# The last regroup in two halves, three PSUM tags in turn for the output units, batches in their own order

## The chip, the cores and the metric

The kernel runs on one core of a Trainium2 chip. The metric is device time in microseconds for one execution, from the runtime's measurement; the profiled execution also has a span, the time from the first to the last event that the profiler recorded on the core. The engines are PE (matmul, with its weight loads as a row of its own, PEld), DVE (VectorE), ACT (ScalarE), POOL (GpSimd) and SP (SyncE, which here only issues transfers). Each engine works through its own instructions in order.

## What is computed

A linear attention (feature map exp(x) and exp(-x) of a projection) over 8 batches, 8 heads, 576 positions, head size 64 gives x of shape (8, 576, 512). Then a Fourier layer mixes it over the positions:

```python
X = np.fft.rfft(x, axis=1)                       # 64 lowest modes are kept
Yr = einsum('bmd,mde->bme', Xr, w_r) - einsum('bmd,mde->bme', Xi, w_i)
Yi = einsum('bmd,mde->bme', Xr, w_i) + einsum('bmd,mde->bme', Xi, w_r)
Y[:, :n_modes] = Yr + 1j * Yi
y = np.fft.irfft(Y, n=S, axis=1)
u = x + y
return (u + np.maximum(u @ w_ch, 0.0)).astype(np.float32)
```

Inputs and output are float32; the kernel works in bfloat16 with float32 sums.

## The kernel before

**Attention, and the weights.** 32 steps of attention fill `xs_all` (the attention's output, 5 chunks of up to 128 positions for each of 8 batches) and, by matmul with a cosine and sine matrix, the modes `XT`. Beside them the mode weights (64 modes of 512 x 512, real and imaginary) are loaded by POOL's queue in 32 groups and multiplied: `mode_mm` sums a group of 8 modes and a quarter of the input width into `psY`, `mode_sum` adds the quarters up in `Yacc`, and for the last quarter writes `yst`. The last ten groups (k = 22 to 31) come after the attention.

**What is done beside the last groups.** For each chunk, x times `w_ch` is wanted later: `flip_x` (L637) transposes a pair of chunks, `times_w` (L647) multiplies by `wchb` and ACT stores the product in `xw`. For ten pairs of chunks, called late, `reordered` (L672) permutes the rows of `xs_all` to the order of the output (a matmul with `ident_p` at L679, a copy by ACT at L681), so that x can be added by POOL at the end instead of by PE. The table `late` says which.

**Regrouping.** After each two groups of the last quarter (P = 0 to 3, 16 modes each) `by_batch` (L684) regroups `sY`, which has modes and batches mixed, by batch. Its matmuls give Z = Y times `w_ch` (`mm_z`, L689, 16 matmuls a half, 32 columns each) and R = Y itself (`mm_r`, L695), four batches a half, each batch in 32 partitions. `copy(j)` moves batches j and j + 4 with one instruction of ACT (Z into `zall`, L705) and one of DVE (R into `yall`, L706). In P = 3 the copies are a list of five steps that the last loop takes one at a time: batch 0 (with the first half's matmuls), batch 4 (with the second half's), then j = 1, 2 and 3; of the last, both copies are ACT's.

**The output units.** The output is made in 20 units. A unit has two chunks (`half` False: 128 rows each, 1024 numbers in each partition) or the 64-row fifth chunks of two batches (`half` True, 512 numbers). A unit runs so:

- `add_xw` (L760): PE puts `xw` into the PSUM tile `psB` (2 matmuls);
- `add_z` (L768): PE adds the inverse transform of `zall` (2 matmuls, L771), then ACT writes Relu(psB) into the output tile `of` (L773);
- `spec` (L775): PE puts x into `psA` (2 matmuls, L780; left out in a late unit) and adds the inverse transform of `yall` (2 matmuls, L783); DVE adds psA to `of` (L786); in a late unit POOL then adds x from `xs_all` to `of` (L790);
- SP issues the stores (L824): 64 partitions each, so two for a unit.

PSUM is held as four tags T0 to T3 of two banks, all eight banks together; a tile of a tag waits until the readers of the tag's last tile are done. psZ and psR of P = 3 hold T0 and T1. Units 0 to 3 take T2 for psB and T3 for psA each time; from unit 4 on even units take (T2, T3) and odd ones (T0, T1). The units go by b = 0 to 3: the chunks of batch b and of batch b + 4, then their fifth chunks (in b = 3 these come first). The stores of a unit that is not late are issued right after it, those of a late unit two units later (`LAG`). An output tile holds four chunks of a batch and has one of three buffers of tag w0 or w1.

Of the kernel before, what the change touches and what calls it, by code (L numbers as in the profile page):

```python
# [10 lines left out]
F32 = mybir.dt.float32  # L11
# [7 lines left out]
B_, H_, S_, D_ = 8, 8, 576, 64  # L19
NMODES = 64  # L20
DMODEL = 512
NCH = 5
# [4 lines left out]
def kernel(  # L27
# [11 lines left out]
    nc = tc.nc  # L39
# [4 lines left out]
    psum = psum_cm.__enter__()  # L44
    pw = ctx.enter_context(tc.tile_pool(name="pw", bufs=3))
# [10 lines left out]
    Yacc = pers.tile([128, 8, DMODEL], F32, name="Yacc")  # L56
# [93 lines left out]
    def weights(k):  # L150
        g, gi = groups[k]
        wt = {}
        for ri, w in ((0, moe_w_r), (1, moe_w_i)):
            t = pw.tile([128, 8, DMODEL], BF16, name=f"w{'ri'[ri]}", tag=f"w{ri}")
            if gi >= 0:
                nc.gpsimd.dma_start(  # L156
                    t, w[8 * gi:8 * gi + 8, g * 128:(g + 1) * 128, :].rearrange("m p e -> p m e"))
            else:
                for x in range(2):
                    mx = 16 * (-1 - gi) + 8 * x  # L160
                    nc.gpsimd.dma_start(
                        t[64 * x:64 * x + 64],
                        w[mx:mx + 8, g * 64:(g + 1) * 64, :].rearrange("m p e -> p m e"))
            wt[ri] = t
        W[k] = wt
# [252 lines left out]
    def mode_sum(k, psY, pb=None):  # L418
        g, gi = groups[k]
        if gi < 0:  # L420
            G = -1 - gi
            if g == 0:
                nc.vector.tensor_copy(Yacc[:, 2 * G:2 * G + 2, :], psY)
            else:
                nc.vector.tensor_tensor(
                    out=Yacc[:, 2 * G:2 * G + 2, :], in0=psY, in1=Yacc[:, 2 * G:2 * G + 2, :],
                    op=ALU.add)
        elif g < 3:
            nc.vector.tensor_tensor(  # L429
                out=Yacc[:, gi, :], in0=psY, in1=Yacc[:, gi, :], op=ALU.add)  # L430
        else:
            yst = pb.tile([128, DMODEL], BF16, name="yst", tag="yst", bufs=2)
            nc.vector.tensor_tensor(out=yst, in0=psY, in1=Yacc[:, gi, :], op=ALU.add)
            return yst
# [82 lines left out]
    with tc.manual_schedule():  # L517
# [15 lines left out]
        for n in range(N + 2):  # L533
# [60 lines left out]
            e = n - (N + 2 - N_EARLY)  # L594
# [28 lines left out]
    psum = ctx.enter_context(tc.tile_pool(name="psumT", bufs=1, space=bass.MemoryType.PSUM))  # L623
# [4 lines left out]
    yall = pb.tile([128, B_, DMODEL], BF16, name="yall", bufs=1)  # L628
    zall = pb.tile([128, B_, DMODEL], BF16, name="zall", bufs=1)
# [3 lines left out]
    todo = list(range(N_EARLY, B_ * NCH, 2))  # L633
    ahead = []
    copies = []
# [11 lines left out]
    def times_w():  # L647
        i, sT = ahead.pop(0)
        ps = psum.tile([128, 2, DMODEL], F32, name="psW", tag="T2")
        for x in range(2):  # L650
            for dc in range(4):
                nc.tensor.matmul(ps[:, x, :], lhsT=sT[:, x, dc, :], rhs=wchb[:, dc, :],  # L652
                                 start=(dc == 0), stop=(dc == 3))
        nc.scalar.copy(xw[:, i - N_EARLY:i + 2 - N_EARLY, :], ps)  # L654

    def pieces(n):
        for _ in range(n):
# [7 lines left out]
                copies.pop(0)()  # L665


    late = {0: ((1, 0), (1, 2)), 1: ((0, 0), (1, 0), (1, 2)), 2: ((0, 0), (1, 0), (1, 2)),
            3: ((0, 0), (0, 2))}
    reorder = sorted((b + 4 * x) * NCH + c for b in range(4) for x, c in late[b])  # L670

    def reordered(tag):  # L672
        i = reorder[0]
# [9 lines left out]

    def by_batch(sY, P):  # L684
        cols = [sY[:, dc].rearrange("p g c -> p (g c)") for dc in range(4)]
        psZ = psum.tile([128, 2, DMODEL], F32, name="psZ", tag="T0")
        psR = psum.tile([128, 2, DMODEL], F32, name="psR", tag="T1")

        def mm_z(h):  # L689
            for dc in range(4):  # L690
                for j in range(4):
                    nc.tensor.matmul(psZ[32 * j:32 * j + 32, h, :], lhsT=cols[dc][:, j + 4 * h::8],
                                     rhs=wchb[:, dc, :], start=(dc == 0), stop=(dc == 3))

        def mm_r(h):  # L695
            for dc in range(4):
                for j in range(4):
                    nc.tensor.matmul(
                        psR[32 * j:32 * j + 32, h, dc * 128:(dc + 1) * 128],
                        lhsT=cols[dc][:, j + 4 * h::8], rhs=ident_b, start=True, stop=True)  # L700

        def copy(j, h=None, one=False):
            r = slice(32 * j, 32 * j + 32)
            bs, hs = (slice(j, None, 4), slice(0, 2)) if h is None else (j + 4 * h, h)
            nc.scalar.copy(zall[32 * P:32 * P + 32, bs, :], psZ[r, hs, :])  # L705
            (nc.scalar.copy if one else nc.vector.tensor_copy)(  # L706
                yall[32 * P:32 * P + 32, bs, :], psR[r, hs, :])

        if P < 3:
            for f in (mm_z, mm_r):  # L710
                for h in range(2):
                    f(h)
            copies.extend([lambda j=j: copy(j) for j in range(4)])
        else:

            copies.extend([lambda: (mm_z(0), mm_r(0), copy(0, 0)),
                           lambda: (mm_z(1), mm_r(1), copy(0, 1)),
                           lambda: copy(1), lambda: copy(2), lambda: copy(3, None, True)])

    with tc.manual_schedule():  # L720
        plan = {22: 3, 23: 3, 24: 2, 25: 2, 26: 2, 27: 1, 28: 2, 29: 1, 30: 1, 31: 0}
        while k_out < 32:
            k = k_out
            gi = groups[k][1]
            while k_in < min(k_out + NW, 32):
                weights(k_in)
                k_in += 1
            yst = mode_sum(k, mode_mm(k, "T3"), pb)
            k_out += 1
            if yst is not None:  # L730
                if ahead:
                    times_w()
                pt = psum.tile([128, 4, 128], BF16, name="ptY", tag="T3")
                for dc in range(4):
                    nc.tensor.transpose(pt[:, dc, :], yst[:, dc * 128:(dc + 1) * 128], ident_b)
                if gi % 2 == 0:
                    sY = pb.tile([128, 4, 2, 128], BF16, name="sY", tag="sY")
                nc.vector.tensor_copy(sY[:, :, gi % 2, :], pt)
                if gi % 2 == 1:
                    by_batch(sY, gi // 2)  # L740
            pieces(plan[k])
            if k <= 24 or k % 2 == 0:
                assert not copies
                for tag in ("T0", "T1"):
                    if reorder:
                        reordered(tag)
            if k == 30:
                times_w()
        assert not todo and not ahead and not reorder and len(copies) == 5

# [37 lines left out]
            nc.gpsimd.tensor_tensor(out=o, in0=o, in1=xs_all[:, i:i + 2, :], op=ALU.add)  # L790

    units = []
    for b in range(4):
        of = [pw.tile([128, 4, DMODEL], F32, name="of", tag=f"w{x}") for x in range(2)]
        o4 = Yacc[:, 2 * b, :]
        us = []
        for x in range(2):
            out_v = out[b + 4 * x].rearrange("(p n) e -> p n e", n=9)
            for c in (0, 2):
                us.append(dict(bc=((b + 4 * x, c), (b + 4 * x, c + 1)), o=of[x][:, c:c + 2, :],  # L800
                               late=(x, c) in late[b], half=False,
                               dmas=[(out_v[:, 5 * jj + c:5 * jj + c + 2, :],
                                      of[x][jj::2, c:c + 2, :]) for jj in range(2)]))
        u4 = dict(bc=((b, 4), (b + 4, 4)), o=o4, late=False, half=True,
                  dmas=[(out[b + 4 * x].rearrange("(p n) e -> p n e", n=9)[:, 4, :],
                         o4[64 * x:64 * x + 64]) for x in range(2)])
        units += [u4] + us if b == 3 else us + [u4]

    with tc.manual_schedule():
        LAG = 2  # L810
        copies.pop(0)()
        for n in range(len(units) + LAG):
            if n < len(units):
                u = units[n]
                u["tags"] = ("T2", "T3") if n % 2 == 0 or n < 4 else ("T0", "T1")
                add_xw(u)
                add_z(u)
                spec(u)
                if copies:
                    copies.pop(0)()  # L820
            for lag, is_late in ((LAG, True), (0, False)):
                if 0 <= n - lag < len(units) and units[n - lag]["late"] == is_late:
                    for dst, src in units[n - lag]["dmas"]:
                        nc.sync.dma_start(dst, src)  # L824

# [29 lines left out]
```

## Time and profile before

| what | us |
|---|---|
| median of 3 runs (lowest, highest) | 462.61 (461.35, 463.44) |
| the profiled execution | 463.39 |
| its span | 461.6 |
| first to last issue of a store (L824) | 422.3 to 457.9 |

Busy time, out of the span: PE 312.4, DVE 298.8, ACT 264.5, POOL 196.3. The transfers' engines are near full until the last weights have come, at about 415 us, and are used in part from there on; the page's second part shows it slice by slice (the last six slices, of 11.5 us each, moved 207, 140, 63, 146, 318 and 293 GB/s). Busy shares over the span say little about the last 45 us; the timeline and windows of that part are what to read.

### The profile page before, as it was taken

To read this page: it belongs to the slowest core of one execution; us is meant where nothing else is said; L and a number is where in the kernel's file an instruction comes from. 1 tells how busy PE (TensorE), PEld (TensorE's weight loads), DVE (VectorE), ACT (ScalarE), POOL (GpSimd) and SP (SyncE) were. 2 spreads that over 40 slices of the span, in tenths; PEclk is the share of its full clock that TensorE was granted. 3 is DMA by queue.
4 is the path that set the end of the run, shared out by engine and by line. 5 is a ranking of instruction groups with operands and counts; after the bars stand their busy time and mean duration, and the time that the engine had idled before them with its cause. 6 is when DMAs were issued, how large, how long until landed. Compare 5 with 4: busy or idle time off the path is not lost.

```text
span 461.6 us, 11115 instructions
## 1 busy us (share of the span) xinstructions
PE 312.4 (68%) x4637; PEld 202.2 (44%) x4637; DVE 298.8 (65%) x418; ACT 264.5 (57%) x531; POOL 196.3 (43%) x246
## 2 busy tenths in 40 slices
PE   1676777745675777667465655576678878868893
PEld 1464655623454555534343433344344544433341
DVE  5688799856988789876555473776322274465674
ACT  3766876743676877855555453756233445655662
POOL 4596395545564256644344332533022113000583
PEclk9997798886978669986678585989799999999898
DMA  8999999999999999999999999999999999981488
GB/s 170 262 254 241 237 218 217 229 206 219 221 225 218 229 218 222 221 223 224 218 208 223 213 218 219 207 208 207 207 207 207 207 207 207 207 140 63 146 318 293
DMA packets 84577, 99.08 MB, mean 215 GB/s; under 512 B 3504, under 2 KB 75824, under 8 KB 84528
## 3 DMA queue, kind: packets, MB, share of 16 engines
q0 software_dynamic: 73872, 74.72, 97.3%
q1 hardware_dynamic: 10496, 23.60, 15.7%
q8 instruction: 36, 0.59, 0.5%
q14 instruction: 13, 0.11, 0.1%
q10 hardware_dynamic: 160, 0.07, 0.1%
HBM read 163.64 MB, written 9.44 MB: 375 GB/s over the span
## 4 chain that ended last, share of the span: by engine, by line
DMA 26%; DVE 25%; issue 19%; PE 16%; ACT 6%; POOL 5%; SPq 2%; DVEq 0%; ACTq 0%; POOLq 0%
DMA wi<-in_moe_w_i_dram 20%; DVE mkq L227 7%; DVE xs_all L330 4%; DMA q<-in_q_dram 4%; DVE nd L316 3%; DVE tB L309 3%; ACT AA L234 3%; PE psNB L299 2%; ACT e L256 2%; PE ptr L178 2%; DVE of L786 2%; SPq L123 2%; DMA kn<-in_k_dram 2%; PE psB L764 1%; POOL vaug L264 1%
## 5 line engine op out<-in xcount | busy, mean ns | idle before, releaser
L264 POOL TENSOR_TENSOR vaug<-vn,ee 128x576 bf16<-128x576 f32 x64 | 72.6, 1152 | 59.9 <-ACT ee L249 53.9
L234 ACT ACTIVATE AA<-psT 128x1024 bf16<-128x1024 f32 x64 | 62.0, 1021 | 44.0 <-PE psT L202 43.5
L156 POOL DMA_DIRECT2D wr<-in_moe_w_r_dram x24 | 21.8, 908 | 115.5 <-PE psY L410 108.3
L256 ACT ACTIVATE e<-mkq 64x4 f32<-64x4 f32 (+1 forms) x128 | 26.4, 206 | 65.8 <-DVE mkq L227 63.5
L238 ACT ACTIVATE AA<-psk 128x1024 bf16<-128x1024 f32 x64 | 61.4, 1009 | 0.0
L410 PE MATMUL psY<-wi,XT 128*32 128x512 bf16 x192 | 25.3, 472 | 25.5 <-DMA wi<-in_moe_w_i_dram 25.5
L410 PEld LDWEIGHTS <-XT 128*32 128x32 bf16 x384 | 17.8, 167 | 51.0 <-issue 42.6
L227 DVE TENSOR_REDUCE mkq<-psk 128x8 f32<-128x1024 f32 x32 | 38.8, 1213 | 1.3 <-PE psk L193 1.3
L790 POOL TENSOR_TENSOR of<-of,xs_all 128x1024 f32<-128x1024 f32 x10 | 21.1, 2130 | 42.2 <-DVE of L786 42.2
L227 DVE TENSOR_REDUCE mkq<-psq 128x8 f32<-128x1024 f32 x32 | 38.9, 1216 | 0.1
L654 ACT CAST xw<-psW 128x1024 bf16<-128x1024 f32 x17 | 17.2, 1013 | 36.4 <-PE psW L652 36.4
L429 DVE TENSOR_TENSOR Yacc<-psY,Yacc 128x512 f32<-128x512 f32 x16 | 11.0, 690 | 40.8 <-PE psY L410 40.7
L184 DVE COPY kT<-ptr 128x640 bf16<-128x640 bf16 x32 | 15.7, 492 | 29.6 <-PE ptr L178 29.6
L410 PE MATMUL psY<-wr,XT 128*32 128x512 bf16 x192 | 24.7, 473 | 14.9 <-DMA wr<-in_moe_w_r_dram 6.4
L280 PE MATMUL kvz<-vaug,AA 64*128 64x65 bf16 x1152 | 29.5, 211 | 7.4 <-POOL vaug L269 5.9
L309 DVE TENSOR_TENSOR tB<-psNB,e 128x650 f32<-128x650 f32 x32 | 26.7, 833 | 11.4 <-PE psNB L299 10.7
L299 PEld LDWEIGHTS <-AA 128*128 128x128 bf16 x640 | 30.3, 113 | 8.3 <-issue 7.7
L652 PE MATMUL psW<-wchb,sT 128*128 128x512 bf16 x136 | 32.2, 379 | 2.1 <-ACT xw L654 2.1
L330 DVE TENSOR_TENSOR xs_all<-nd,rden 128x640 bf16<-128x640 f32 x32 | 30.8, 964 | 1.1
L280 PEld LDWEIGHTS <-AA 64*128 64x128 bf16 x1152 | 25.2, 107 | 12.3 <-issue 8.3
L178 PE MATMUL ptr<-ident_b,k 128*128 128x128 bf16 x160 | 18.4, 263 | 17.2 <-DVE qT L184 16.5
L316 DVE TENSOR_TENSOR nd<-psNA,tB 128x650 f32<-128x650 f32 x32 | 26.7, 835 | 4.1 <-DVE tB L309 0.5
(128 smaller groups left out, 719.6 us busy)
## 6 DMA issues: line engine op xcount, KB each, us to landing
wr<-in_moe_w_r_dram POOLq DMA_DIRECT2D x24, 1024.0 KB, 23.3
wi<-in_moe_w_i_dram POOLq DMA_DIRECT2D x24, 1024.0 KB, 27.5
wr<-in_moe_w_r_dram POOLq DMA_DIRECT2D x16, 512.0 KB, 18.2
wi<-in_moe_w_i_dram POOLq DMA_DIRECT2D x16, 512.0 KB, 20.5
out_dram<-of SPq DMA_DIRECT2D x32, 256.0 KB, 2.4
vn<-in_v_dram SPq DMA_DIRECT2D x24, 288.0 KB, 5.7
q<-in_q_dram POOLq DMA_DIRECT2D x12, 288.0 KB, 19.2
k<-in_k_dram POOLq DMA_DIRECT2D x12, 288.0 KB, 20.2
```

Of the source, the lines that this page charges most:

```text
L227: nc.vector.tensor_reduce(out=o, in_=i, axis=AX.X, op=ALU.max, apply_absolute_value=True)
L234: nc.scalar.activation(AA[:, 0, ab, 0:1024].rearrange("f (x j p) -> f j x p", j=2, p=64), st["psT"].rearrange("f j (x p) -> f j x p", p=64 ...
L238: nc.scalar.activation(AA[:, 1, ab, 0:1024].rearrange("p (c j f) -> p j c f", c=4, j=2), st["psk"], ACT.Exp, scale=sc)
L256: nc.scalar.activation(e2[64 * jj:64 * jj + 64, hh, 0:NCH - jj], mkq[64 * hh:64 * hh + 64, 1, 5 * jj:5 + 4 * jj], ACT.Exp, scale=2.0)
L264: nc.gpsimd.tensor_tensor(out=vaug[:, ab, :, 0:64], in0=st["v"], in1=ee[:, ab, :].unsqueeze(2).to_broadcast([128, 9, D_]), op=ALU.mult,)
L280: nc.tensor.matmul(kvz[:, hh, ab * 65:(ab + 1) * 65], lhsT=AA[r, 1, ab, 128 * j:128 * j + 128], rhs=vaug[r, ab, j, :], start=(j == 0), sto ...
L299: nc.tensor.matmul(p[:, hh, 65 * c:65 * c + 65], lhsT=AA[:, 0, ab, x:x + 128], rhs=kvzF[:, hh, ab * 65:(ab + 1) * 65], start=True, stop=True,)
L309: nc.vector.tensor_tensor(out=tB, in0=st["psNB"], in1=e2.unsqueeze(3).to_broadcast([128, 2, NCH, 65]), op=ALU.mult,)
L316: nc.vector.tensor_tensor(out=nd, in0=st["psNA"], in1=st["tB"], op=ALU.add)
L330: nc.vector.tensor_tensor(out=xo, in0=nd[:, :, :, 0:64], in1=rden.to_broadcast([128, 2, NCH, 64]), op=ALU.mult,)
L410: nc.tensor.matmul(psY[32 * j:32 * j + 32, :], lhsT=XT[:, c0:c0 + 32, m], rhs=wt[ri][:, 2 * j + par, :], start=(par == 0 and ri == 0), sto ...
L652: nc.tensor.matmul(ps[:, x, :], lhsT=sT[:, x, dc, :], rhs=wchb[:, dc, :], start=(dc == 0), stop=(dc == 3))
```

## The change

Nothing before P = 3 changes but the table `late`, which holds other chunks (still ten pairs). After it:

- the last regroup is in two halves: `make(h)` makes one tile `psL` of tag T0, with Z of four batches in its first bank and R in its second. The second half's matmuls come when batch 4 is first wanted, after the eighth unit. `copy_one(b)` moves one batch: Z by ACT, R by DVE, or by ACT in batches 3, 5 and 7. There are eight steps of copies, taken one batch ahead of need;
- the units go in the order of the batches 0 to 7, with the fifth chunks of two batches after each odd batch;
- psB and psA take tags T1, T2, T3 in turn: the tile numbered s = 2n + x takes T(1 + s mod 3);
- the stores of batches 1 to 5 are of four chunks (two stores of 512 KB a batch), issued after the batch's last unit; the others stay at two chunks. Each unit has its own lag: 3 if late, 1 if it closes a batch of 1 to 5 with a unit that is not late, 0 otherwise. There are 30 stores in place of 40.

```diff
-    late = {0: ((1, 0), (1, 2)), 1: ((0, 0), (1, 0), (1, 2)), 2: ((0, 0), (1, 0), (1, 2)),
-            3: ((0, 0), (0, 2))}
-    reorder = sorted((b + 4 * x) * NCH + c for b in range(4) for x, c in late[b])
+    late = {(b, 0) for b in range(1, B_)} | {(2, 2), (4, 2), (6, 2)}
+    reorder = sorted(b * NCH + c for b, c in late)
...
-            copies.extend([lambda: (mm_z(0), mm_r(0), copy(0, 0)),
-                           lambda: (mm_z(1), mm_r(1), copy(0, 1)),
-                           lambda: copy(1), lambda: copy(2), lambda: copy(3, None, True)])
+            last = {}
+
+            def make(h):
+                last[h] = ps = psum.tile([128, 2, DMODEL], F32, name="psL", tag="T0")
+                mm_z(h, ps[:, 0, :])
+                mm_r(h, ps[:, 1, :])
+
+            def copy_one(b):
+                r = slice(32 * (b % 4), 32 * (b % 4) + 32)
+                ps = last[b // 4]
+                nc.scalar.copy(zall[rows, b, :], ps[r, 0, :])
+                (nc.scalar.copy if b in (3, 5, 7) else nc.vector.tensor_copy)(
+                    yall[rows, b, :], ps[r, 1, :])
+
+            for b in range(B_):
+                copies.append(lambda b=b: (make(b // 4) if b % 4 == 0 else None, copy_one(b)))
...
+    for b in range(B_):
+        of = pw.tile([128, 4, DMODEL], F32, name="of", tag=f"w{b % 2}")
+        out_v = out[b].rearrange("(p n) e -> p n e", n=9)
+        whole = 0 < b < 6
+        for c in (0, 2):
+            c0 = 0 if whole else c
+            units.append(dict(bc=((b, c), (b, c + 1)), o=of[:, c:c + 2, :],
+                              late=(b, c) in late, half=False,
+                              lag=3 if (b, c) in late else 1 if whole else 0,
+                              dmas=[(out_v[:, 5 * jj + c0:5 * jj + c + 2, :],
+                                     of[jj::2, c0:c + 2, :]) for jj in range(2)]
+                              if c == 2 or not whole else []))
+        if b % 2:
+            o4 = Yacc[:, b, :]
+            units.append(dict(bc=((b - 1, 4), (b, 4)), o=o4, late=False, half=True, lag=0,
+                              dmas=[(out[b - 1 + x].rearrange("(p n) e -> p n e", n=9)[:, 4, :],
+                                     o4[64 * x:64 * x + 64]) for x in range(2)]))
 
     with tc.manual_schedule():
-        LAG = 2
         copies.pop(0)()
-        for n in range(len(units) + LAG):
+        for n in range(len(units) + 3):
             if n < len(units):
                 u = units[n]
-                u["tags"] = ("T2", "T3") if n % 2 == 0 or n < 4 else ("T0", "T1")
+                u["tags"] = [f"T{1 + (2 * n + x) % 3}" for x in range(2)]
                 add_xw(u)
                 add_z(u)
                 spec(u)
-                if copies:
+                if copies and 8 - len(copies) <= u["bc"][0][0] + 1:
                     copies.pop(0)()
-            for lag, is_late in ((LAG, True), (0, False)):
-                if 0 <= n - lag < len(units) and units[n - lag]["late"] == is_late:
+            for lag in (3, 1, 0):
+                if 0 <= n - lag < len(units) and units[n - lag]["lag"] == lag:
                     for dst, src in units[n - lag]["dmas"]:
                         nc.sync.dma_start(dst, src)
```

## The prediction, made before the changed kernel had run

> **What bounds the kernel now.** I read the chain of waits first, in order of time, then the timeline of the last 45 us engine by engine, then the granted clock in stretches of 3.4 us. The chain:
>
> ```profile
> 391.35 23.62 DMA wi<-in_moe_w_i_dram
> ...
> 415.96 0.70 DVE yst L433
> ...
> 424.17 1.24 DVE of L786
> 425.41 0.04 issue
> 425.45 0.61 PE psA L783 x2
> ...
> 442.83 0.43 PE psB L764 x2
> 443.26 0.43 PE psB L771 x2
> 443.69 0.43 PE psA L783 x2
> ```
>
> Up to 415 us the kernel waits for its last weights. Nothing before that changes except which rows L679 permutes (ten pairs before, ten after, one a step earlier: two matmuls and a 1.01 us ACT copy, hidden under the 23.62 us load and priced at nothing; without that cover it would be 0.43 + 1.01 us). So the tail decides, from the copy of the last sY (ends 417.58) to the end at 461.6. Two regimes: an opening (424 to 431) in which PE and DVE alternate, and a stretch from 431.5 on in which PE runs back to back.
>
> ```profile
> 430.47 0.64 PE L780 MATMUL psA<-xs_all,ident_b 128*64 128x512 bf16 x2 [1.37 <-DVE of L786]
> 435.68 0.59 PE L764 MATMUL psB<-xw,ident_p 128*128 128x512 bf16 x2
> 436.74 1.02 ACT L773 ACTIVATE of<-psB 128x1024 f32<-128x1024 f32 x1 [0.70 <-PE psB L771]
> 437.80 2.52 DVE L786 TENSOR_TENSOR of<-psA,of 128x1024 f32<-128x1024 f32 x2 [0.50 <-ACT of L773]
> ...
> 451.35 4.21 POOL L790 TENSOR_TENSOR of<-of,xs_all 128x1024 f32<-128x1024 f32 x2 [1.03 <-DVE of L786]
> 452.02 1.20 SPq L824 DMA_DIRECT2D out_dram<-Yacc  x2
> 453.50 4.99 SPq L824 DMA_DIRECT2D out_dram<-of  x8
> ```
>
> From these rows: Relu starts 1.06 after a unit's first matmul (435.68 to 436.74) and takes 1.02; the add follows 0.04 later and takes 1.23 alone; so a unit's add ends 3.35 after its first matmul. The last row is the end of the kernel: eight stores issued in one run on SP, the last at 457.89 (L824's rows run from 422.3 to 457.9), 0.63 apart; the span ends 3.7 later. Whatever moves the start of that run moves the end.
>
> ```profile
> 410.20:413.60 3.40, 2.07 (x10) 1.00 0.59 98
> 413.60:417.10 3.50, 1.96 (x22) 1.00 0.05 9
> ...
> 427.30:430.70 3.40, 1.43 (x9) 0.97 0.15 63
> 430.70:434.10 3.40, 3.40 (x11) 0.53 0.55 192
> 434.10:437.50 3.40, 3.40 (x18) 1.00 0.56 194
> ```
>
> Columns: stretch, length, PE busy (instructions), granted clock, DMA share, GB/s. After the one stretch in which PE was busy 42% the clock is halved for 3.4 us, which costs 1.7 us of PE work; after 56% and 61% it is not.
>
> **The change part by part.** *PE work* is the same: ten late units of 6 matmuls x 0.216 = 1.30, six others of 8 x 0.216 = 1.73, four half units of 1.27 (438.36 to 439.63), and twice the 32 small matmuls (1.26: 417.63 to 418.89).
>
> *Opening.* Before, the first four units share one pair of PSUM tags and the second half's matmuls and two-batch copies (1.22 on DVE, 1.00 on ACT) stand among them: first psB at 418.89, sixth at 431.47, 12.58 us. After, three tags rotate, so tile s takes the tag of tile s-3: psB of unit n waits for the add of unit n-2, psA of unit n for the Relu of unit n-1. Copies are of one batch (0.57 ACT, 0.68 DVE). A small loss: Z and R now share one tile, so the first z copy waits for R's matmuls too (419.01 for 418.77) and DVE's copy waits for ACT's (419.62 for 419.01). Laying it out with the durations above, first matmuls fall at 418.90, 420.91, 422.64, 424.55 (waits for the second unit's add), 426.38, and the sixth at 428.01 (waits for the fourth's add): 9.11 us, 3.46 less, of which 1.26 is the second half's matmuls put off.
>
> *Fifteen later units.* Now the price of three tags: S(n+2) >= S(n) + 3.35 + 0.04, that is 1.70 a unit, where a late unit needs only 1.30 of PE. Before, it was psA, 0.86 later, that waited for the add two units back: (3.39 - 0.86)/2 = 1.27 a unit, under 1.30, and the rows from 435 on show no idle PE. First matmuls after: 428.01, 429.30, 431.41 (add), second half 432.92, 434.24, 436.06; 437.64 (add), 438.93, 441.03 (add), 443.28 (add), 445.11; 446.68 (add), 447.98, 450.08 (add), 452.33 (add), 454.16. The waits at 443.28 and 452.33 are longest since for batches 5 and 7 both copies run on ACT (2 x 0.57) ahead of the Relu that the add needs. PE work from 428.01 on: 9 x 1.30 + 3 x 1.73 + 3 x 1.27 + 1.3 = 22.0, against 27.0 laid out: 5.0 us of waits. Before, 431.47 to 454.0 is 22.5 and holds no such waits, only the 1.7 of halved clock. After, PE is never under 76% busy in a 3.4 us stretch, so by the five rows I expect no halving in the tail.
>
> Behind a waiting psB stand all later matmuls in order, the second half's and its own psA's among them; ACT and DVE then wait for those.
>
> The Trainium skill ("Perfetto Trace Analysis", section Matmul Optimizations) speaks against three tags: it wants all eight PSUM banks in use, and after the change the units rotate through six; the page has no price, only the layout above gives one. On the clock, the Trainium skill ("TensorE: Matmul & The Clock Gate", section "What's actually happening") says the gate's 3.4 us window runs free and halves the clock after an idle one; here 42% busy was enough, and by the page's wording the 1.7 us would not be in the time before and the loss would be 3.9 instead of 2.2.
>
> *The end.* The add of the 19th unit (batch 7, c=2) ends at 452.33 + 1.07 + 1.06 + 1.23 = 455.69. SP stands at that unit's store, in order, with the stores of (6,2), o4 and (7,0) behind it, although the Pool add of (6,2) is done at 454.5: again eight issues in one run, from 455.73 instead of 453.50. Pool's last add (454.52 to 456.64) is done before its turn. Last issue 455.73 + 7 x 0.63 = 460.1, for 457.89: **+2.2 us**.
>
> *Stores.* 40 become 30; ten carry 512 KB. No row has such a store; 128 KB and 256 KB ones issue in 0.571 and 0.570, so I take 0.57; the other end is doubling with the bytes, 1.14. Either way nothing: the last large pair is issued near 447.6, and SP next waits until 452.28 (a Pool add). Landing: 256 KB took 2.4, at 410 GB/s twice that is 3.0; bounded above by the 1024 KB loads' 27.5, which would hold only the reuse of an output buffer. I take 3.0. The bytes are no bound: 9.44 MB / 410 GB/s = 23 us of some 36.
>
> *Sum:* opening -3.46, later units 27.05 - 22.5 = +4.5, end of PE +1.0; the run of stores starts one unit's Relu and add behind PE rather than behind a Pool add, +1.2 more. Span 461.61 + 2.2 = 463.8; with 1.78 around it (463.39 measured for this execution) **465.6**. That execution lies 0.8 over the median 462.61. I do not take the 0.8 off: the halved stretch hangs on one 3.4 us window, so other executions may lack it (463.39 - 1.6 = 461.8), and what I lay out for after has none in either case. The same layout applied to before, with the halved stretch put in, gives the last add at 454.43 (row: 454.36) and the last issue within 0.1 us.
>
> **Unknown costs.** Restart of PE after a wait: the rows show 0.04; PEld's waits on issue up to 0.8. At ten waits, 0 to +1.0; I take 0.04 each. Tags freed earlier than the add's recorded end: -1.4 if a third of the 5.0 goes. The level of the median: -0.8 to 0.
>
> **Rivals.** (1) *Not slower:* three tags hold PE less than I count, since Relu and add pipeline closer. For: in the opening the same three tags are a gain. Against: each wait is one PSUM tile with one reader whose end is a row. With no waits 465.6 - 5.0 = 460.6; it decides from waits under 2.8 us (0.19 a unit instead of 0.33). (2) *The halved clock comes in the tail after too,* since some window falls on a wait: a cycle's 0.86 doubles and the next is late by a little, +1.1: 466.7. Against: 76%. (3) *The offset of the profiled execution carries over* (halved clock or not is the same in all executions): 462.61 + 2.2 = 464.8, which is within 0.5%, about what a measurement of this kernel can tell from no change. (4) *The change does nothing it says*, because stores limit the end: against, the stores before the last run had gaps of SP (452.0, then 453.5).
>
> **How the numbers follow.** Forecast 0.62 (time 464.9 to 466.4); rival 1 0.08 (0.05 faster, 0.03 not), rival 2 0.08, rivals 3 and 4 0.22. Slower by over 0.5% (464.9): 0.62 + 0.08 = 0.70; within: 0.22 + 0.03 = 0.25; faster 0.05. Range: 465.6 - 0.8 - 1.4 = 463.4 to 465.6 + 1.1 + 0.6 of restarts = 467.3.
>
> **What would show it.** PE waits for "DVE of" at L775 in about every second unit, some 5 us in all; a sixth first matmul near 428; no clock below 0.9 between 418 and 455; a last run of eight stores from about 455.7. Wrong if PE runs back to back from 428 on, or if the last stores start before 453.5.

## The result, and the profile after

The changed kernel takes 466.07 us (median of 12 executions, 463.52 to 469.58), the kernel before 462.69 (median of 12 beside it, 461.11 to 464.65). The ratio is 1.0074, 95% interval 1.0051 to 1.0098: slower by about 3.4 us. The profiled execution took 466.13, with a span of 464.4.

Two profiles can't be subtracted end to end here, because the last weights arrive at another time in each execution (414.97 before, 416.33 after, though the code that loads them is the same). So everything below is counted from the end of the last copy of `sY`, where the tail begins: 417.58 before, 418.93 after. "Tail" is from there to the issue of the last store. It is 40.3 before and 42.1 after; to the end of the span 44.0 and 45.4. Of the 2.7 us between the two profiled executions (463.39 and 466.13), then, 1.4 lie ahead of the tail and 1.4 in it.

First the chain of waits after, in order of time (start, length, what):

```profile
392.17 24.16 DMA wi<-in_moe_w_i_dram
...
443.10 1.24 DVE of L797
444.33 0.04 issue
444.38 0.59 PE psB L775 x2
444.97 0.45 PE psB L782 x2
445.41 0.02 issue
445.44 1.03 ACT of L784
446.47 0.02 issue
446.49 1.24 DVE of L797
```

Where the chain of before ran through PE alone at this place, it now goes round: add, first matmul two units later, Relu, add. The timeline of PE after shows the same as waits (start, length, what, idle time before and what ended it):

```profile
438.86 0.59 PE L775 MATMUL psB<-xw,ident_p 128*128 128x512 bf16 x2 [0.52 <-DVE of L797]
440.15 0.59 PE L775 MATMUL psB<-xw,ident_p 128*128 128x512 bf16 x2
442.25 0.59 PE L775 MATMUL psB<-xw,ident_p 128*128 128x512 bf16 x2 [0.64 <-DVE of L797]
444.38 0.59 PE L775 MATMUL psB<-xw,ident_p 128*128 128x512 bf16 x2 [0.67 <-DVE of L797]
```

From 438.86 to 442.25 are 3.39 us for two units, as the prediction's layout had it (3.35 + 0.04). And SP's timeline at the end: stores, then a hole, then a run of eight from 456.67 on.

```profile
453.34 1.12 SPq L836 DMA_DIRECT2D out_dram<-of  x2
456.67 1.11 SPq L836 DMA_DIRECT2D out_dram<-of  x2
...
459.16 1.18 SPq L836 DMA_DIRECT2D out_dram<-Yacc  x2
460.44 1.18 SPq L836 DMA_DIRECT2D out_dram<-of  x2
```

The clock of after, in stretches of 3.41 us laid so that the changes of clock in its trace fall on their ends (stretch, length, PE busy with its instructions, granted clock, DMA share, GB/s). The emptiest stretch of its later units has PE busy 2.10 of 3.41, and the clock is halved only after the stretch in which the last matmuls end:

```profile
441.30:444.71 3.41, 2.10 (x10) 1.00 0.85 310
...
454.95:458.36 3.41, 1.22 (x10) 1.00 0.42 167
458.36:461.78 3.42, 0.00 (x0) 0.50 0.97 332
```

### The profile page after: what moved, and what is told of

It is laid out like the page before. It is cut to its first block, busy times and chain, and to the rows that moved or that the text cites. A ratio compares the mean times of both kernels' runs of the same rounds, so it can differ in the third digit from the quotient of the medians.

```text
span 464.4 us, 11105 instructions
## 1 busy us (share of the span) xinstructions
PE 305.5 (66%) x4637; PEld 198.0 (43%) x4637; DVE 299.6 (65%) x419; ACT 264.9 (57%) x536; POOL 196.9 (42%) x246
## 4 chain that ended last, share of the span: by engine, by line
DMA 31%; DVE 24%; issue 18%; PE 11%; ACT 7%; POOL 6%; SPq 1%; POOLq 1%; DVEq 0%; ACTq 0%
DMA wi<-in_moe_w_i_dram 20%; DVE mkq L227 7%; DMA k<-in_k_dram 5%; DMA q<-in_q_dram 4%; DVE xs_all L330 4%; DVE nd L316 3%; DVE tB L309 3%; ACT AA L234 2%; POOL vaug L264 2%; DVE of L797 2%; DMA kn<-in_k_dram 2%; ACT of L784 2%; SPq L123 1%; ACT e L256 1%; PE ptr L178 1%
## 5 line engine op out<-in xcount | busy, mean ns | idle before, releaser
L410 PEld LDWEIGHTS <-XT 128*32 128x32 bf16 x384 | 17.8, 167 | 54.9 <-issue 45.4
L429 DVE TENSOR_TENSOR Yacc<-psY,Yacc 128x512 f32<-128x512 f32 x16 | 11.0, 689 | 42.8 <-PE psY L410 42.7
L330 DVE TENSOR_TENSOR xs_all<-nd,rden 128x640 bf16<-128x640 f32 x32 | 32.8, 1025 | 1.1
L299 PEld LDWEIGHTS <-AA 128*128 128x128 bf16 x640 | 28.0, 108 | 9.5 <-issue 9.1
L202 PE MATMUL psT<-qT,w 64*128 64x512 bf16 x64 | 15.1, 462 | 23.0 <-DVE mkq L227 23.0
```

The lines of the kernel that those rows point to most:

```text
L299: nc.tensor.matmul(p[:, hh, 65 * c:65 * c + 65], lhsT=AA[:, 0, ab, x:x + 128], rhs=kvzF[:, hh, ab * 65:(ab + 1) * 65], start=True, stop=True,)
L330: nc.vector.tensor_tensor(out=xo, in0=nd[:, :, :, 0:64], in1=rden.to_broadcast([128, 2, NCH, 64]), op=ALU.mult,)
L410: nc.tensor.matmul(psY[32 * j:32 * j + 32, :], lhsT=XT[:, c0:c0 + 32, m], rhs=wt[ri][:, 2 * j + par, :], start=(par == 0 and ri == 0), sto ...
```

## The experiments

Each is one edit of one of the two kernels unless it says more. The tails of all, from their profiles:

| kernel | tail | to the end of the span | halved clock that overlaps the tail, up to the last matmul |
|---|---|---|---|
| before | 40.3 | 44.0 | 430.5 to 433.9 |
| before, second profile | 38.7 | 42.4 | none |
| after | 42.1 | 45.4 | none |
| store order | 40.9 | 44.2 | none |
| fourth tag | 41.2 | 44.8 | 417.8 to 421.2 |
| copies on DVE | 41.8 | 45.1 | none |
| small stores | 42.1 | 45.8 | none |
| before, three tags | 42.7 | 46.4 | 431.4 to 434.8 |
| four tags, more edits | 40.2 | 43.7 | 416.1 to 419.5 |
| one store a unit | 39.3 | 43.7 | 416.6 to 423.4 |
| filled wait | 38.5 | 42.1 | none |
| no fill | 40.5 | 44.2 | 415.9 to 422.8 |
| after, filled wait | 42.1 | 45.4 | none |

### The price of three tags alone, in the kernel before

```diff
-                u["tags"] = ("T2", "T3") if n % 2 == 0 or n < 4 else ("T0", "T1")
+                u["tags"] = ("T2", "T3") if n < 4 else [f"T{1 + (2 * n + x) % 3}" for x in range(2)]
```

> The kernel before with one edit: from the fifth unit on psB and psA take T1, T2, T3 in turn instead of the pairs (T2, T3) and (T0, T1). Opening, copies, order and stores are those of before. Theory: this is the price of three tags alone, PE waits for the add two units back in the later units: tail 40.3 (before, with a stretch of halved clock) or 38.7 (before without it) plus 2.4, time +2 to +3 us on before. Rival, that the three tags cost nothing and the loss came from the order of batches and copies: tail and time as before. Also a second look at the opening of before: by the theory of the clock a halved stretch appears in it only where a 3.4 us stretch falls on the waits, in about a third of the executions.

Tail 42.7: 2.4 over the 40.3 of before, and like it with a halved stretch in the opening. The median is 465.12 beside 463.13 of before; the ratio, 1.0018 (0.9985 to 1.0051), does not separate them, so the verdict rests on the trace. Its PE waits where before's ran through. Three units of before, then three of this run:

```profile
440.94 0.59 PE L764 MATMUL psB<-xw,ident_p 128*128 128x512 bf16 x2
442.66 0.59 PE L764 MATMUL psB<-xw,ident_p 128*128 128x512 bf16 x2
443.96 0.59 PE L764 MATMUL psB<-xw,ident_p 128*128 128x512 bf16 x2
```

```profile
444.27 0.59 PE L764 MATMUL psB<-xw,ident_p 128*128 128x512 bf16 x2 [0.21 <-DVE of L786]
445.56 0.59 PE L764 MATMUL psB<-xw,ident_p 128*128 128x512 bf16 x2
447.66 0.41 PE L764 MATMUL psB<-xw,ident_b 128*64 128x512 bf16 x2 [0.64 <-DVE of L786]
```

The order of batches, the copies and the stores are before's here, so the waits are the tags'. The rival, that the tags cost nothing, falls.

### A fourth tag for the second half of the units, in the kernel after

```diff
+                u["tags"] = ([f"T{1 + (2 * n + x) % 3}" for x in range(2)] if n < 10 else
+                             [("T3", "T0"), ("T1", "T2")][n % 2])
...
+                for _ in range(2 if n in (8, 9) else 1):
+                    if copies and (8 - len(copies) <= u["bc"][0][0] + 1 or n in (8, 9)):
```

> The changed kernel, but the copies of batches 5, 6 and 7 are made right after the ninth and tenth unit, and from the eleventh unit on psB and psA rotate over four tags, with T0. Theory, that three tags hold PE for about 0.33 us a unit: from the eleventh unit on PE runs without waiting for DVE, tail 42.1 - 2.0 = 40.1, time about 464.0. Rival, that DVE and ACT are the bound of the later units and tags are not: the bunched copies only delay the next Relu, tail 42.1 or more.

Median 463.60, 1.0009 of before (0.998 to 1.0038). The tail is 41.2, not 40.1: a halved stretch from 417.8 to 421.2 delayed its second unit by 1.0 (423.29 where after had 422.29, with its tail begun at the same time within 0.04 us), which is most of the 1.1. So the code of the changed kernel, too, has executions with a halved clock at the head of its tail: up to the ninth unit this run differs from it in nothing. The bunched copies also cost a wait, 1.2 us of PE for the last copy by ACT. But from the eleventh unit on:

```profile
442.50 0.59 PE L775 MATMUL psB<-xw,ident_p 128*128 128x512 bf16 x2
443.79 0.59 PE L775 MATMUL psB<-xw,ident_p 128*128 128x512 bf16 x2
445.09 0.59 PE L775 MATMUL psB<-xw,ident_p 128*128 128x512 bf16 x2
446.91 0.41 PE L775 MATMUL psB<-xw,ident_b 128*64 128x512 bf16 x2
447.89 0.60 PE L775 MATMUL psB<-xw,ident_p 128*128 128x512 bf16 x2
```

1.30 a late unit and no wait in brackets: DVE and ACT, whose work here is the same, were not the bound, the tags were.

### The order of the last stores

```diff
-                              lag=3 if (b, c) in late else 1 if whole else 0,
+                              lag=3 if (b, c) in late else 1 if whole or b == 7 else 0,
```

> One edit of the changed kernel: the stores of unit (7, c=2) are issued one unit later, after those of (6, c=2). Measure: from the end of the last copy of sY to the issue of the last store (the tail), 42.1 us in the profile of the changed kernel. My theory, that SP's queue stood at the store of (7, c=2) while a finished unit waited behind it: the run of stores starts two issues earlier, tail 40.9, last run before the end six stores instead of eight, time about 1.2 us under the changed kernel (about 464.8). Rival, that the stores' bytes or POOL's last add set the end: tail 42.1, no change of time.

Tail 40.9, as the theory had it to a tenth; median 465.07, ratio to before 1.0027 (0.9988 to 1.0066). SP's end:

```profile
453.84 4.53 SPq L836 DMA_DIRECT2D out_dram<-of  x6
458.48 1.19 SPq L836 DMA_DIRECT2D out_dram<-Yacc  x2
459.76 1.18 SPq L836 DMA_DIRECT2D out_dram<-of  x2
```

Its last add and POOL's last add end 38.3 and 38.6 after the last copy of sY, just as in the changed kernel, and yet its last store is issued 1.2 us sooner. So the queue's order was worth 1.2 us by itself, by the traces; the ratios to before (1.0027 here, 1.0074 for the changed kernel) have intervals that overlap. One part of the expectation failed: the last run has eight issues as in the changed kernel, not six. It begins at 455.98 (two of the row's six were issued ahead of it, from 453.84 on), 36.5 after the last copy of sY, where the changed kernel's begins 37.7 after it.

### Copies of batches 5 and 7 on DVE

```diff
-                (nc.scalar.copy if b in (3, 5, 7) else nc.vector.tensor_copy)(
+                (nc.scalar.copy if b in (3,) else nc.vector.tensor_copy)(
```

> The changed kernel, but R of batches 5 and 7 is copied by DVE instead of ACT. Theory, that the waits before the fourteenth and nineteenth unit are longer because two ACT copies stand before the Relu which the add needs: each gets shorter by the second copy, 0.5 us, half of it given back where DVE's 0.68 is in the way: tail 41.5. Rival, that DVE is the tighter engine: tail 42.1 to 43.

Tail 41.8: 0.3 won, half of what was expected, and seen in the trace alone; median 465.61, ratio 1.0054 (1.0026 to 1.0082). The timelines say why. First the twelfth unit in after, then in this run: the copies of batch 5, the Relu (ACT L784) and the add (DVE L797) which the fourteenth unit waits for.

```profile
440.96 0.57 ACT L724 CAST zall<-psL 32x512 bf16<-32x512 f32 x1
441.45 0.57 ACT L725 CAST yall<-psL 32x512 bf16<-32x512 f32 x1
442.04 1.02 ACT L784 ACTIVATE of<-psB 128x1024 f32<-128x1024 f32 x1
443.10 2.49 DVE L797 TENSOR_TENSOR of<-psA,of 128x1024 f32<-128x1024 f32 x2 [0.90 <-ACT of L784]
```

```profile
439.69 0.57 ACT L724 CAST zall<-psL 32x512 bf16<-32x512 f32 x1
440.29 1.02 ACT L784 ACTIVATE of<-psB 128x1024 f32<-128x1024 f32 x1
440.95 0.69 DVE L725 CAST yall<-psL 32x512 bf16<-32x512 f32 x1
441.67 1.23 DVE L797 TENSOR_TENSOR of<-psA,of 128x1024 f32<-128x1024 f32 x1
```

Counted from the first copy, the Relu starts 0.48 sooner (0.60 for 1.08), which is the 0.5 that was expected. But the add starts only 0.16 sooner (1.98 for 2.14): DVE is busy with its copy until 441.64, 0.33 after the Relu has ended. More was given back than the half that was counted.

### Stores of 256 KB in the middle again

```diff
-        whole = 0 < b < 6
+        whole = False
```

> The changed kernel with each unit's own stores of 256 KB in all batches (40 stores again, lags as in its batches 0, 6 and 7). Theory: the longer stores are worth nothing either way, since SP waits before the last run in both: tail 42.1, to the end of the span 45.5. Rival, that the longer stores delay the last run or relieve it: off by over 0.5 us.

Tail 42.1, to the end of the span 45.8: no difference in the tail. One execution, 465.08 us. The end follows the last issue by 3.7 here and by 3.3 in after, though both end with the same eight stores; no run says why. The larger stores changed the issues, though. These are SP's half-unit stores in after, and then in this kernel (shortest, median and longest issue in ns):

```profile
L836 SPq DMA_DIRECT2D out_dram<-Yacc x8: 543/1093/1197, 430.8 to 459.7; - x8
```

```profile
L836 SPq DMA_DIRECT2D out_dram<-Yacc x8: 543/576/610, 429.2 to 458.3; - x8
```

Behind the stores of 512 KB the issue of a 128 KB one takes up to twice as long. That costs no tail here, since SP then waits for an add.

### A second profile of the kernel before

> The kernel before, unchanged: a second look at its opening. Theory of the clock: where no 3.4 us stretch of the waits at 424 to 431 has PE under about half busy, no halved stretch follows, and from the end of the last copy of sY to the last store's issue it is 38.7 us, to the end of the span 42.4, instead of 40.3 and 44.0. Where the halving comes again, 40.3 and 44.0 again. Rival, that the 1.7 us is not the clock's: 40.3 without a halved stretch.

One execution, 461.67 us. No halved stretch in the tail, tail 38.7 and 42.4 to the end of the span, both as expected. The waits of the opening are the same as in the first profile; only the grid of 3.41 us stretches lies otherwise (they end at 414.57, 417.99 and so on, by this trace's changes of clock), and no stretch of the grid is empty enough:

```profile
424.81:428.23 3.42, 2.08 (x9) 1.00 0.38 153
428.23:431.64 3.41, 2.04 (x14) 1.00 0.14 56
```

61% and 60% busy, and no halving. In the first profile one stretch of the grid had the whole of the waits, 42%, and the next was halved:

```profile
427.07:430.48 3.41, 1.44 (x10) 1.00 0.22 88
430.48:433.89 3.41, 3.41 (x10) 0.50 0.50 180
```

That took 1.6 us. Against the unhalved tail of before the change costs 42.1 - 38.7 = 3.4 us up to the last issue, and 45.4 - 42.4 = 3.0 to the end of the span; against the halved one 1.8 and 1.4. The medians differ by 3.4. How many executions of before are halved was not counted, so the medians can't be split further.

### Towards a faster version

The runs above say: keep the halves and small copies of the opening, free T0 early, and mind the queue's order. The first version has four edits of the changed kernel:

```diff
+    late = {(b, 0) for b in range(1, 7)} | {(2, 2), (4, 2), (6, 2)}
...
+                              lag=3 if (b, c) in late else 1 if whole or b == 7 else 0,
...
+                u["tags"] = ([f"T{1 + (2 * n + x) % 3}" for x in range(2)] if n < 8 else
+                             [("T2", "T0"), ("T3", "T1")][n % 2])
...
+                if copies and n < 7:
                     copies.pop(0)()
```

> The changed kernel with four edits: one batch's copies after each of the first seven units, so that the second half comes after the fourth unit and T0 is free from the ninth on, psB and psA then over four tags; the stores of (7, c=2) one unit later; and unit (7, c=0) not late (nine pairs are permuted instead of ten, PE adds x there). Theory: PE waits only in the first nine units, tail 37.7, to the end of the span 41.9; time 466.1 - 3.6 = 462.5, no worse than before. Rival, DVE and ACT bound the later units: tail over 40.

Median 463.33, 1.0014 of before (0.9983 to 1.0046): the time that after lost is mostly back. The tail, 40.2, is 2.5 over what was expected; a halved stretch from 416.1 on is part of it, the rest was not separated. The rival's number (over 40) came out as well, but not its reason: PE's last wait for an add is ahead of the ninth unit, and from the tenth on its timeline shows none, so DVE and ACT did not bound the later units.

Then one store for a unit of two chunks, over all 128 partitions, with `whole = False` and a lag of 2 for late units:

```diff
+                              dmas=[(bass.AP(tensor=out_v.tensor,
+                                             offset=out_v.offset + c0 * DMODEL,
+                                             ap=[[9 * DMODEL, 64], [5 * DMODEL, 2],
+                                                 [1, (c + 2 - c0) * DMODEL]]),
+                                     of[:, c0:c + 2, :].rearrange("p c e -> p (c e)"))]
```

> As the run with four tags for all later units, but one store for a unit of two chunks in place of two (both halves of the partitions in one transfer of 512 KB), issued at once, or two units later if the unit is late; no store of four chunks. Theory: 24 issues at 0.6 us instead of 30, the last run is no longer bound by issues but by the bytes at 410 GB/s: to the end of the span 40.7 from the last copy of sY, time 466.1 - 4.8 = 461.3, about 0.3% under before. Rival: an issue takes longer with twice the rows, then 41.9 as in the other.

Median 462.54, 0.9985 of before (0.9954 to 1.0015): not told apart from before. To the end of the span 43.7 instead of 40.7, with 6.8 us of halved clock from 416.6 on. The rival, that an issue takes longer with twice the rows, is not what the rows show: the sixteen stores of 512 KB were issued in 0.54 to 0.64 us each, but for one of 0.94. It was the second of each two 128 KB stores behind them that took 1.20 to 1.23.

So the next one went back to two stores of 256 KB a unit, and put five matmuls that nobody reads into the wait for the last weights:

```diff
+                if k == 31 and par == 0 and ri == 0:
+                    fill = psum.tile([128, DMODEL], F32, name="fill", tag="T0")
+                    for _ in range(5):
+                        nc.tensor.matmul(fill, lhsT=ident_b, rhs=wchb[:, 0, :],
+                                         start=True, stop=True)
```

> As the run with four tags for all later units, with each unit's own two stores of 256 KB (at once, or two units later if it is late), and with five matmuls of 128x512 whose product nobody reads in the wait for the last weights, between the first four matmuls of the last group and the four that need those weights. Theory: the issue of a store no longer lasts over 0.61 us; the 3.4 us stretch before the tail has PE over half busy, so no halved stretch at 414 to 423 as in the two runs before, whose tails it lengthened by 1 to 2 us. Tail about 38.0, to the end of the span 41.0, time 461.5, 0.25% under before. Rival: the wait is longer than the five matmuls can fill in many executions, or they delay the last group by up to 1 us, and nothing is gained: time 462.5.

Median 461.42, **0.9978 of before (0.9957 to 0.9999)**: this version beats both kernels, the one before by a margin just clear of the noise, the changed one, by the two ratios to before, by some 4.4 us. Tail 38.5; to the end of the span 42.1, 1.1 more than expected. Its clock is whole until the last stores. Its tail is only 0.2 us shorter than the unhalved one of before (38.7), so most of the 1.0 us between the medians lies elsewhere, perhaps in executions of before with a halved clock, which no run counts; the five matmuls were not tried in the kernel before. The timeline of PE shows the five in the wait, done before the weights are there:

```profile
412.53 1.25 PE L419 MATMUL fill<-wchb,ident_b 128*128 128x512 bf16 x5
414.83 0.48 PE L410 MATMUL psY<-wi,XT 128*32 128x512 bf16 x4 [1.04 <-DMA wi<-in_moe_w_i_dram]
```

Last, the same version without the five, and the changed kernel with them:

> The fastest version so far (four tags, early copies, 256 KB stores, nine late pairs) without the five matmuls in the wait for the last weights. Theory: those keep the clock whole at the head of the tail, which without them is halved in about half of the executions for 3.4 us: median 0.5 to 0.8 us more, 462.0 to 462.2; where the profile shows a halved stretch between 414 and 424, the tail is about 1 to 1.5 us over 38.5. Rival: the five matmuls do nothing and the small stores made the gain: 461.4, tail 38.5.

Median 463.19, 1.0004 of before (0.9983 to 1.0025). The five matmuls were worth 1.8 us by the two medians, 1.2 us by the two ratios to before, whose intervals overlap; 0.5 to 0.8 was expected. The traces show what they did. The stretches of the clock without them, then with them:

```profile
412.51:415.92 3.41, 0.91 (x12) 1.00 0.13 22
415.92:419.34 3.42, 2.47 (x28) 0.50 0.02 5
419.34:422.75 3.41, 3.41 (x28) 0.50 0.00 0
```

```profile
412.59:416.01 3.42, 2.10 (x19) 1.00 0.06 10
416.01:419.42 3.41, 2.26 (x38) 1.00 0.02 5
```

Without them PE is busy 27% of the stretch ahead of the tail, then follows half the clock from 415.9 to 422.8, and a tail 2.0 us longer (40.5 for 38.5). With them the same stretch has PE busy 61%, and the clock stays whole.

> The changed kernel with the same five matmuls in the wait for the last weights and nothing else. Theory: the tail stays at 42.1 where no halved stretch fell in it before; the executions in which one did are gone, median 465.5. Rival, that the matmuls delay the last weights' group: 466.5 or more.

Median 465.76, 1.0079 of before (1.0054 to 1.0104); tail 42.1. In the changed kernel they gain nothing that this measurement can tell: its own waits on the tags remain, and its first profile had no halving to remove. Single executions still spread, from 464.5 to 468.7 in six.

## Why the prediction was right

*The forecast*, 465.6 with slower at 0.70, met 466.07. The mechanism, waits of PE on three tags and a late last run of stores, is what the runs show. That the number came so close is in part luck: in the profiles the end of the span moved by 1.4 us from the last copy of sY on, where 2.2 was summed, and another 1.4 came ahead of the tail, which the sum had at nothing.

*The opening.* The sixth unit's first matmul was laid out 10.43 after the last copy of sY (428.01 - 417.58) and came 10.46 after it (429.39 - 418.93); in the kernel before it was 13.89. The gain of 3.46 is there (3.43). Some 0.4 of it is the halved stretch of before, which began ahead of the sixth unit: in its second, unhalved profile that unit came after 13.45.

*The three tags.* 5.0 us of waits were counted from the sixth unit on; the view of waits has nine of PE for the add, 5.4 us, of which the seven behind the sixth unit make 4.3. The kernel before with three tags and the changed one with four show the cause from both sides. Rival 1, that PE would not be held, is out.

*The last run of stores.* Laid out 38.15 after the last copy of sY, it began 37.74 after it (456.67 - 418.93); before, 35.92. The 0.4 is a mis-sized term of the later units: the fourteenth and the nineteenth unit came 0.12 sooner each than laid out (two ACT copies counted at 2 x 0.57 take 0.49 + 0.57), and the ninth, behind the second half's matmuls, 0.17 sooner. The tail grew by 1.8 where 2.2 was summed. The end of the span moved less still, by 1.4, since it follows the last issue by 3.3 instead of 3.7. That the last run carries 1.8 MB instead of 2.1 is not shown to be the reason: with the small stores the same run ends 3.7 after its last issue.

*The clock.* That the halved stretch belongs to some executions only was what kept the forecast at 465.6 instead of 464.8. The second profile of before shows it: 38.7 without halving, and the medians differ by 3.4, near the 3.0 between the unhalved tails, taken to the end of the span. Rival 3, the same offset in all executions, would have been right with a measured 464.8 and falls with that profile. Rival 2, halving by the tag waits in the changed kernel's tail, was not seen in its profile nor in those of its four variants with the same three tags (store order, copies on DVE, small stores, filled wait). Its margin was smaller than laid out, though: the emptiest stretch has PE busy 62%, not 76%. And "none in either case" was too much: the profile with the fourth tag had a halved stretch at the head of its tail, from the wait for the last weights, in code that is still the changed kernel's.

*The stores.* The price of nothing was right; the reason was half wrong. The issue of a 512 KB store was put at 0.57, with 1.14 as the other end; nine of the ten took 0.47 to 0.60 and one 1.20, and the 128 KB stores behind them up to 1.20. In the range, a third of the 5.0 us of waits is 1.7, not the 1.4 that was taken off.

*Not settled:* why single executions of the changed kernel spread from 463.5 to 469.6; those of before spread as widely (460.8 to 467.5 in the 31 beside the first experiments). The stretch before the tail differs by 1.9 us between profiles of the same code: with the changed kernel's code up to there the tail begins at 417.5 to 419.4 (six profiles), with before's at 417.2 to 417.6 (three). Whether the change makes it begin later is open.

## What to carry to other kernels

With tiles of a unit rotating over buffers, write down for each tile which reader frees it: at three tags the first tile of a unit waited for the last reader two units back, at four only the second tile stands behind it, and that alone was 1.70 instead of 1.30 us a unit. Read a queue in its order at the end of a kernel: one store waiting for its unit kept a finished one behind it, 1.2 us. And count a gap in PE's work by what follows it too: here a stretch of 3.41 us with PE busy 27% halved the clock of the work behind it, and five cheap matmuls that raised it to 61% kept the clock whole.

## What the runs showed of the hardware

The clock is decided on a grid of 3.41 us stretches that lies differently in each execution: in every one of the 13 traces all changes of the granted clock are a whole number of such stretches apart. 42%, 27% and 26% busy in one were followed by half the clock, 60% and 61% were not. Counted over all stretches at full clock up to the last matmul, in all traces: of the 110 with PE busy under 40% all were followed by half the clock, of the 793 with 60% or more none, and of the 272 between them 125. The way back asks for more: of the stretches at half clock, none of the 110 with PE busy under 70% was followed by the full clock, all of the 167 with 95% or more were, and of the 145 between them 68. So it is that the stretch from 415.92 on above, 72% busy, is followed by a second one at half clock.

The Trainium skill, "TensorE: Matmul & The Clock Gate", section "What's actually happening", has the free-running stretch of this length, and the runs agree; it halves the clock after an idle stretch, and here a stretch that was 42% busy was enough.

SP's issue of a store of 64 rows of 4 KB took 0.47 to 0.61 us in the kernel before; behind stores of 512 KB, in the changed kernel, the issue of a 128 KB store took up to 1.20.
